# Spreading the third pair's decay factors between two products of the first y, from an eight-row operand on GpSimd's queue

## Chip, cores and metric

One NeuronCore of one Trainium2 chip runs the whole kernel. The metric is the device time in microseconds (us) of one execution. It was taken in three runs, and one further execution was recorded by the hardware profiler. Engine names are those of the profile: PE is TensorE (PEld its weight loads), DVE VectorE, ACT ScalarE, POOL GpSimd, SP SyncE, which here only issues DMAs.

## What is computed

A chunked state-space product (Mamba-2) is followed by a feed-forward block with a sigmoid-type gate. The reference, cut to what matters (4 batches b, 8 heads h, 768 steps, chunks of 32 in the reference, head size 32, state size 16; then 3072 tokens of width 256, hidden width 2048):

```python
log_a = np.log(np.clip(a, 1e-06, 1.0))
for c in range(nc):
    cum = np.cumsum(la, axis=-1)
    L = np.exp(cum[:, :, :, None] - cum[:, :, None, :]) * causal
    CB = np.einsum('bhin,bhjn->bhij', Cc, Bc)
    y_intra = np.einsum('bhij,bhjd->bhid', CB * L, xc)
    y_inter = np.einsum('bhin,bhnd->bhid', Cc, state) * decay_to_i
    y[:, :, sl] = y_intra + y_inter
    state = decay_full * state + sum_j(Bc x xc * decay_from_j)
x = y.transpose(0, 2, 1, 3).reshape(3072, 256)
h = x @ w_in                      # 256 x 2048
g = h * (1.0 / (1.0 + np.exp(-1.702 * h)))
out = g @ w_out                   # 2048 x 256
```

`x, a, B, C` are float32; `w_in` and `w_out` are float64 and come into the kernel as pairs of 32-bit words.

## The kernel before

The 3072 tokens are worked off in six groups of 512 (TG), each of four blocks of 128 steps (a batch has six such blocks, NC = 6; CG = 4). Two blocks make a pair, so that there are twelve pairs and a group has two (PG = 2). A block is cut into two chunks of 64. All engines follow one written order: the program is emitted in the order in which it shall run, and `in_order` at the end pins each engine's instructions to it. Nothing is rescheduled afterwards, so what is late on an engine holds up everything behind it.

**Decay factors.** For a pair, VectorE makes L, the running products of a within a chunk, with one scan along the free axis. The scan needs a, with a zero at each chunk's first step, copied to every partition ("spread"). Pairs 0 and 1 go another way: log a is summed up (`cum`), TensorE forms the differences and ScalarE takes the exp. Pairs 3 and later read a spread by DMA from `scratch` (`spread`). The third pair, number PG = 2, is spread by TensorE. `pick_a` (ScalarE, L375) copies a's rows twice, scaled by a column of zeros and ones, so that each quarter of the partitions holds two heads and zero elsewhere. `fan_all` (L421) then multiplies with ones, eight products into the four PSUM banks `ab2`, which `decay_fanned` scans (L464).

For the state's decay from the batch's start, `since`, the rows of a are needed once per state row. For batch 0's first four blocks they come from the exp of `cum`; for its last two, `fan_since` has TensorE repeat them by a matrix of zeros and ones, `whose` (L515), and repeat each chunk's first value too (L544), and `since_fanned` scans these from PSUM (L555, L557). For the later batches a DMA copies the rows to 16 partitions each (`spread_rows`), `clip_rows` clips them on VectorE and moves the first values with GpSimd, and `decay_rows` scans.

**Order of the start.** TensorE: products that keep it busy (L454), the masks (L562), the differences (L568), a few small products as padding (`pads(11)`, L446), transposes (L641), the scores of pairs 0 and 1 (L696) with the rows for `since` (L526) between them, the chunk sums (L727), a filler (L1178), then the first y: the chunk products of pair 0 (L850), a filler product of 192 columns into the area `idle` (L1178), the chunk products of pair 1 (L850) and those with the state (L836). ScalarE copies y to `yT` (L870).

**First hidden layer.** `hidden(0, f)` for f from 0 to 15 (L907) multiplies yT with block f of w_in: two products of 512 columns, each of which TensorE runs as two records with a weight load each; ScalarE applies Silu. After block f the entries of `in_hidden[0][f]` are emitted: the work of other engines for later. There the float64 words are turned into float32 weights piece by piece: `fields` (L192, L195) and `rounded` (L208) on VectorE, `clamp` on ScalarE (L203, L204), `join` on VectorE (L222, L228). `narrow(i)` does this for piece i. Piece 4 holds blocks 8 to 11, piece 5 blocks 12 to 15, later pieces w_out. After block 5 `store_a` clips a and stores it to `scratch`, after block 7 comes `pick_a(2)`, after block 9 `fan_all(2)`. In `narrow(4)` stands the clip of a's last two blocks (L360, L366, L367), in `narrow(6)` the scan `since_fanned`.

**Then** group 0 is multiplied with w_out (`project_all`, L1004), with the scores, chunk sums and y of pairs 2 and 3 between (L696, L727, L836, L850, at places 10 and 15). `turn` transposes B and C of pairs 2 and 3 by TensorE, and `since_start` (L681) multiplies C with `since` into CsT. From group 1 on both layers are done with fewer products by Strassen-Winograd's scheme (L962, L972, L1067, L1074; sums on VectorE at L930 and L1094, copies on ScalarE at L967, Silu at L939).

**PSUM.** `bank` takes one of four single banks in turn, used by h, o, tp, A and the rows; `area` is one tile of four banks, used in turn by ab0, cb0, `idle`, ab2, cb2 and so on.

**DMA queues.** SyncE issues nearly all DMAs in program order. Its semaphores are used in a ring of eight: an issue waits until the DMA eight issues earlier has landed. `rows_a` loads a's 32 rows (batch and head) four times, once for each quarter of the partitions (L279), behind the pieces of w_in.

**GpSimd** makes the constant masks at the start (`pick0`, `ident`, `below`, `same`, `pick`, `whose`), the masked C of pairs 0 and 1 (L664, `mask_first`), CsT of pairs 0 and 1 (L681), and small moves later. The second L664 waits for a memset on VectorE (L663) that stands behind the first `fields`.

Of the kernel before, what the change touches and what calls it, by code (L numbers as in the profile page):

```python
# [8 lines left out]
FP32 = mybir.dt.float32  # L9
# [3 lines left out]
ALU = mybir.AluOpType  # L13
# [3 lines left out]
P = 128  # L17
# [18 lines left out]
def kernel(  # L36
# [70 lines left out]
        "p (c s) -> p c s", c=NC)  # L107
    az0 = ffn.tile([P, TG // 2], FP32, tag="b", name="az0").rearrange("p (c s) -> p c s", c=2)
    cum = const.tile([P, 2, P], FP32, name="cum")
    w_in = const.tile([P, NF, NK, P], FP32, name="w_in")  # L110
# [164 lines left out]
    def rows_a(t, queues):  # L275

        e = t.shape[1] * P
        for r in range(R):
            queues[r % len(queues)].dma_start(  # L279
                out=t[32 * r:32 * r + 32].rearrange("p c s -> p (c s)"),  # L280
                in_=a.rearrange("b h s -> (b h) s")[:, :e])

# [72 lines left out]

    starts, fans, flat = {}, {}, {}

    def clip(t, name):
# [3 lines left out]
        if name:  # L362
            starts[name] = const.tile([P, t.shape[1], 2], FP32, name=f"starts{name}")
        first = t.rearrange(by_chunk, s=2)[:, :, :, 0]
        if name:
            nc.vector.tensor_copy(starts[name], first)  # L366
        nc.vector.memset(first, 0.0)  # L367

    def pick_a(p):

        b, c = divmod(2 * p, NC)
# [17 lines left out]
    for i, n, head in ((0, 1, PG), (1, 2, PG), (0, 0, 1)):  # L389
        t = whose[32 * i:32 * i + 32, n:n + 1]  # L390
        nc.gpsimd.affine_select(out=t, in_=t, pattern=[[-1, 1], [-head, NH], [0, N]],
                                compare_op=ALU.is_equal, fill=0.0, base=-max(n - 1, 0),
                                channel_multiplier=1)
# [98 lines left out]
    def clip_rows(b):  # L492
        t = raf[b]
        nc.vector.tensor_scalar(out=t, in0=t, scalar1=1e-6, scalar2=1.0,
                                op0=ALU.max, op1=ALU.min)
        first = ssd.tile([P, NC, P], FP32, tag="first", name=f"first{b}", bufs=1)
        nc.gpsimd.memset(first, 0.0)
        f, t0 = (v.rearrange(by_chunk, s=2)[:, :, :, 0] for v in (first, t))
        nc.gpsimd.tensor_copy(f, t0)
        nc.gpsimd.memset(t0, 0.0)  # L500
        firsts[b] = first

    def decay_rows(b):

        t, first = raf.pop(b), firsts.pop(b)
        since[b] = ssd.tile([P, NC, P], FP32, tag="since", name=f"since{b}")
        nc.vector.tensor_tensor_scan(
            out=since[b].rearrange("p c s -> p (c s)"), data0=t.rearrange("p c s -> p (c s)"),
            data1=first.rearrange("p c s -> p (c s)"),
            initial=0.0, op0=ALU.mult, op1=ALU.add)  # L510

    def fan_rows(t, c0, c1, o):

        o = o[:, :(c1 - c0) * P]
        nc.tensor.matmul(out=o, lhsT=whose[:32, 0].rearrange("p h n -> p (h n)"),  # L515
                         rhs=t[:32, c0:c1].rearrange("p c s -> p (c s)"), start=True,
                         stop=True, tile_position=(0, 0), skip_group_check=True)
        return o

    def since_first():  # L520

        since[0] = ssd.tile([P, NC, P], FP32, tag="since", name="since0")
        rows = [bank(f"rows{p}")[:, :2 * P] for p in range(PG)]
        for p in range(PG):
            at = slice(32 * p, 32 * p + 32)
            nc.tensor.matmul(out=rows[p],  # L526
                             lhsT=whose[at, 1 + p].rearrange("p h n -> p (h n)"),
                             rhs=cum[at].rearrange("p k s -> p (k s)"), start=True, stop=True,
                             tile_position=(32 * p, 0), skip_group_check=True)
        for p in range(PG):  # L530
            nc.scalar.activation(since[0][:, 2 * p:2 * p + 2].rearrange("p c s -> p (c s)"),
                                 rows[p], AF.Exp)

    def drops():
# [3 lines left out]
                1).to_broadcast([P, Q * D, 2 * CG - 1]))  # L538

    def fan_since():  # L540
        o = bank("rows4")
        t = fanned["rows"] = fan_rows(az, CG, NC, o)
        f = fanned["starts"] = o[:, 2 * P:2 * P + 2 * (NC - CG)]
        nc.tensor.matmul(out=f, lhsT=whose[:32, 0].rearrange("p h n -> p (h n)"),  # L544
                         rhs=starts[1][:32].rearrange("p c s -> p (c s)"), start=True, stop=True,
                         tile_position=(0, 0), skip_group_check=True)

    fanned = {}

    def since_fanned():  # L550

        t, f = fanned["rows"], fanned["starts"]
        first = ssd.tile([P, NC, P], FP32, tag="first", name="first0", bufs=1)[:, CG:]
        nc.gpsimd.memset(first, 0.0)
        nc.vector.tensor_copy(first.rearrange(by_chunk, s=2)[:, :, :, 0],  # L555
                              f.rearrange("p (c s) -> p c s", s=2))
        nc.vector.tensor_tensor_scan(  # L557
            out=since[0][:, CG:].rearrange("p c s -> p (c s)"), data0=t,
            data1=first.rearrange("p c s -> p (c s)"), initial=0.0, op0=ALU.mult, op1=ALU.add)

# [34 lines left out]
    def bank(name):  # L595
        return ps.tile([P, 4 * P], FP32, tag="ff", name=name)
# [205 lines left out]
    def finish(pairs, steps=range(2)):  # L802
# [98 lines left out]
    def hidden(g, f):  # L901
        j, i = divmod(f, 2)
        if i == 0:
            block(g, j)
        h = bank(f"h{g}_{f}")
        for k in range(NK):
            nc.tensor.matmul(out=h, lhsT=w_in[:, f, k], rhs=yT[g][:, k], start=(k == 0),  # L907
                             stop=(k == NK - 1), skip_group_check=True)

        nc.scalar.activation(gT[g, j][:, i], h, AF.Silu, scale=GELU_SCALE)  # L910
# [285 lines left out]
    fields(0)  # L1196
    mask_first(1)
    to = area("cb0")
    pads(11, to[:, 0])
    turn_back()  # L1200
# [11 lines left out]
    for i in range(2, 6):  # L1212
        fetch(i)
    rows_a(az, (nc.sync,))
    since_start(1, nc.gpsimd)
# [21 lines left out]
    def store_a():  # L1237
        clip(az[:BH, :CG], 0)
        for i, side in enumerate(SIDES):
            nc.sync.dma_start(out=scratch[:, i].rearrange("c r i -> r c i"), in_=az[:32, :, side])  # L1240
# [224 lines left out]
```

## Time and profile before

| what | value |
|---|---|
| median of 3 runs | 348.57 us (348.41 to 349.02) |
| profiled execution | 348.56 us |
| its span, first to last instruction | 346.5 us |
| PE busy | 341.6 us, 99% of the span |
| PEld, DVE busy | 269.1 us (78%), 255.5 us (74%) |
| ACT, POOL busy | 154.9 us (45%), 15.3 us (4%) |
| DMA | 25.92 MB, mean 75 GB/s |
| granted TensorE clock | 1.000 |

The time lies 2.06 us over the span, for what surrounds the first and the last instruction. The busy table of the page adds up instructions of an engine; an engine can be busy all the time and still not set the end, so the table is read beside the chain, which follows the work that ended last back to its start. The timeline lists instructions in order: start, duration, engine, line, operation, output and inputs, count, and in brackets the idle time of the engine before it with what ended that. Instructions of a kind that follow each other stand in one row, and a row's duration runs to the end of its last one. TensorE's instructions are pipelined, so that what counts there is the distance between starts.

### The profile page before, as it was taken

Reading aid. Unit: us, or ns where it says so; the run is one execution under the profiler, and the core shown is the slowest. Engines: PE = TensorE matmul, PEld = TensorE weight load, DVE = VectorE, ACT = ScalarE, POOL = GpSimd, SP = SyncE. Lnnn points to the kernel's source line nnn. Section 1 sums busy time; section 2 is a strip of 40 time slices with the busy share of each in tenths; the row PEclk is TensorE's granted clock in tenths of the full one; section 3 lists DMA queues with packets and bytes.
Section 4 is the critical chain, followed back from the end, with each engine's and each line's share of the span. In section 5 each row is a group of like instructions: output and inputs, shape, how many; then the busy total and the mean of one; then the engine's idle time right before and its main releaser. Section 6 shows DMA issues by size and latency. Waiting matters only on the chain.

```text
span 346.5 us, 8120 instructions
## 1 busy us (share of the span) xinstructions
PE 341.6 (99%) x3378; PEld 269.1 (78%) x3378; DVE 255.5 (74%) x484; ACT 154.9 (45%) x352; POOL 15.3 (4%) x42
## 2 busy tenths in 40 slices
PE   8999999999999999999999999999999999999996
PEld 6634444555788888888888888888888888899996
DVE  5889899998799998857996667788464654465463
ACT  4788771407354323754342554432554321554320
POOL 7300010300000100000000000000000000000000
PEclk9999999999999999999999999999999999999999
DMA  6599899645726100435703037400000400000402
GB/s 159 134 294 222 229 234 123 152 70 97 120 59 125 45 0 11 69 91 97 120 24 53 2 80 122 61 0 3 0 4 3 61 2 0 0 2 0 62 0 61
DMA packets 89981, 25.92 MB, mean 75 GB/s; under 512 B 73433, under 2 KB 87129, under 8 KB 89945
## 3 DMA queue, kind: packets, MB, share of 16 engines
q1 hardware_dynamic: 89112, 24.88, 36.0%
q8 instruction: 26, 0.43, 0.6%
q10 hardware_dynamic: 832, 0.52, 0.5%
q14 instruction: 11, 0.08, 0.1%
HBM read 22.15 MB, written 3.24 MB: 73 GB/s over the span
## 4 chain that ended last, share of the span: by engine, by line
PE 96%; DVE 2%; ACT 1%; issue 0%
PE acc L1067 28%; PE X L962 19%; PE Y L972 14%; PE h L907 9%; PE o L1004 8%; PE acc L1074 7%; PE cb L696 2%; PE y L850 2%; PE y L836 1%; PE A L727 1%; PE ab L568 1%; PE busy L454 1%; DVE L L707 1%; PE ab L562 0%; DVE p L222 0%; DVE steps L749 0%
## 5 line engine op out<-in xcount | busy, mean ns | idle before, releaser
L967 ACT ACTIVATE ac<-X 128x256 f32<-128x256 f32 x76 | 29.1, 383 | 81.5 <-PE X L962 80.8
L1067 PE MATMUL acc<-mg,mw 128*128 128x256 f32 x192 | 54.5, 379 | 0.0
L1094 DVE TENSOR_TENSOR gT<-Y,ac 128x512 f32<-128x512 f32 x38 | 26.2, 689 | 38.1 <-PE Y L972 32.5
L939 ACT ACTIVATE gT<-gT 128x512 f32<-128x512 f32 (+1 forms) x76 | 38.9, 519 | 29.5 <-DVE gT L1094 28.9
L962 PE MATMUL X<-my,mi 128*128 128x256 f32 x152 | 45.2, 380 | 0.0
L1067 PEld LDWEIGHTS acc<-mg,mw 128*128 128x128 f32 x192 | 36.5, 190 | 5.0
L1094 DVE TENSOR_TENSOR gT<-Y,b 128x256 f32<-128x256 f32 x38 | 15.8, 419 | 28.6 <-PE Y L972 28.6
L907 PE MATMUL h<-yT,w_in 128*128 128x512 f32 x80 | 35.6, 597 | 0.7 <-ACT yT L870 0.5
L1067 PE MATMUL acc<-gT,w_out 128*128 128x256 f32 x128 | 35.5, 379 | 0.0
L962 PEld LDWEIGHTS X<-my,mi 128*128 128x128 f32 x152 | 28.0, 190 | 4.1 <-ACT ac L967 0.4
L907 PEld LDWEIGHTS h<-yT,w_in 128*128 128x128 f32 x80 | 14.8, 189 | 19.1 <-issue 15.4
L1004 PE MATMUL o<-gT,w_out 128*128 128x512 f32 x64 | 28.3, 595 | 0.0
L930 DVE TENSOR_TENSOR mg<-gT 128x512 f32<-128x512 f32 x40 | 27.2, 681 | 0.0
L1067 PEld LDWEIGHTS acc<-gT,w_out 128*128 128x128 f32 x128 | 24.2, 190 | 3.4 <-ACT yT L885 0.2
L967 ACT ACTIVATE b<-X 128x256 f32<-128x256 f32 x38 | 14.6, 383 | 21.0 <-PE X L962 20.6
L962 PE MATMUL X<-yT,w_in 128*128 128x256 f32 x76 | 23.2, 389 | 0.0
L972 PE MATMUL Y<-yT,w_in 128*128 128x256 f32 x76 | 22.7, 381 | 0.0
L972 PE MATMUL Y<-my,mi 128*128 128x256 f32 x76 | 22.7, 380 | 0.0
L972 PE MATMUL Y<-yT,mi 128*128 128x256 f32 x76 | 22.5, 379 | 0.0
L962 PE MATMUL X<-my,w_in 128*128 128x256 f32 x76 | 22.4, 379 | 0.0
L1004 PEld LDWEIGHTS o<-gT,w_out 128*128 128x128 f32 x64 | 11.8, 190 | 13.6 <-issue 13.2
L411 DVE TENSOR_TENSOR_SCAN L<-a,idents 128x1024 f32<-128x1024 f32 x9 | 20.5, 2277 | 0.4 <-DMA a<-scratch 0.4
(159 smaller groups left out, 549.7 us busy)
## 6 DMA issues: line engine op xcount, KB each, us to landing
a<-scratch SPq DMA_DIRECT2D x18, 256.0 KB, 5.1
bits<-in_moe_w_out_dram SPq DMA_DIRECT2D x8, 512.0 KB, 7.2
x<-in_x_dram SPq DMA_DIRECT2D x24, 128.0 KB, 3.7
out_dram<-ob SPq DMA_DIRECT2D x40, 64.0 KB, 2.0
bits<-in_moe_w_in_dram SPq DMA_DIRECT2D x8, 256.0 KB, 4.6
bits<-in_moe_w_in_dram SPq DMA_DIRECT2D x4, 512.0 KB, 10.6
b<-in_B_dram SPq DMA_DIRECT2D x20, 64.0 KB, 3.3
af<-in_a_dram SPq DMA_DIRECT2D x3, 384.0 KB
```

The costliest lines, as they stand in the source:

```text
L411: nc.vector.tensor_tensor_scan(out=L, data0=ra[p].rearrange("p k e -> p (k e)"), data1=idents.rearrange("p h i -> p (h i)"), initial=0.0, ...
L696: nc.tensor.matmul(out=s["cb"][side, r, k].rearrange("p (q i) -> p q i", q=Q), lhsT=BT[rows, k, side], rhs=CT[rows, k, :, side], start=Tru ...
L907: nc.tensor.matmul(out=h, lhsT=w_in[:, f, k], rhs=yT[g][:, k], start=(k == 0), stop=(k == NK - 1), skip_group_check=True)
L930: nc.vector.tensor_tensor(out=t[:, 0:2], in0=B[:, :, 1], in1=B[:, 0], op=ALU.subtract)
L939: nc.scalar.activation(o, i, AF.Silu, scale=GELU_SCALE)
L962: nc.tensor.matmul(out=s["X"], lhsT=lhsT, rhs=rhs, start=i == "1", stop=i == "4", skip_group_check=True)
L967: nc.scalar.activation(copy, s["X"], AF.Copy)
L972: nc.tensor.matmul(out=o, lhsT=lhsT, rhs=rhs, start=s.pop("new", False), stop=i != "5", skip_group_check=True)
L1004: nc.tensor.matmul(out=o[c], lhsT=w_out[:, c, f], rhs=gT[g, f // 2][:, f % 2], start=(f == 0), stop=(f == NF - 1), skip_group_check=True)
L1067: nc.tensor.matmul(out=acc[g][0][i][:, cols], lhsT=w, rhs=h[:, cols], start=(j == 0 and k == 0 and (i, 0) in begins), stop=(j == NF // 2 - ...
L1074: nc.tensor.matmul(out=o[k] if type(o) is list else o[:, cols], lhsT=h[:, cols], rhs=w, start=(j == 0 and (i, k) in begins), stop=(j == NF ...
L1094: nc.vector.tensor_tensor(out=o, in0=v, in1=w, op=ALU.add)
```

## The change

The eight products that spread pair 2's factors move from behind hidden block 9 to the first y, in the place of the filler product `idle`. For this their operand must be there about 20 us earlier, and it is made in another way: `az1` is filled with ones, and one DMA on GpSimd's queue brings the eight rows of batch 0's last two blocks to every sixteenth partition. `clip(az1)` clips it on VectorE ahead of the first `fields`, and `pick_a` reads it with a column `pick1`, which VectorE sums from `ident` (L399's kind), in place of GpSimd's `pick`. `pick_a` is now emitted behind `mask_first(1)`.

What `fan_since` did with TensorE goes: `since` for batch 0's last two blocks now comes from `spread_rows(0)` (a DMA of 128 KB), `clip_rows(0)` after block 8 and `decay_rows(0)` in the place of `since_fanned`. The matrix `whose` loses a third, `pick` is gone, a is loaded once and not four times, `store_a` clips all 768 columns at once. Hidden blocks 10 to 12 are multiplied in two halves of 256 columns each. Two of the eleven padding products go.

```diff
 def narrow(i):
-        if i == 4:
-            clip(az[:, CG:], 1)
         if i == 6:
-            since_fanned()
+            decay_rows(0)
...
     def spread_rows(b):
-        raf[b] = raw.tile([P, NC, P], FP32, tag="af", name=f"af{b}", bufs=1)
+        c = CG if b == 0 else 0
+        raf[b] = raw.tile([P, NC, P], FP32, tag="af", name=f"af{b}", bufs=1)[:, c:]
         nc.sync.dma_start(out=raf[b].rearrange("p c s -> p (c s)"),
-                          in_=a[b].unsqueeze(1).to_broadcast([NH, N, S]))
+                          in_=a[b, :, c * P:].unsqueeze(1).to_broadcast([NH, N, S - c * P]))
...
     def pick_a(p):
-            nc.scalar.activation(X[:, :, q], az[:, c:c + 2], AF.Copy, scale=pick[:, b, q:q + 1])
+            nc.scalar.activation(X[:, :, q], az1, AF.Copy, scale=pick1[:, q:q + 1])
+    APART = P // NH
+    nc.gpsimd.memset(az1, 1.0)
+    nc.gpsimd.dma_start(
+        out=az1.rearrange("(h e) c s -> h e (c s)", e=APART)[:, 0], in_=a[0, :, TG:])
...
-    pick = picker("pick", NB, 1, NH)
-    whose = const.tile([32 * PG, 1 + PG, NH, N], FP32, name="whose")
+    whose = const.tile([32 * PG, PG, NH, N], FP32, name="whose")
...
+    pick1 = const.tile([P, Q], FP32, name="pick1")
+    nc.vector.tensor_reduce(
+        out=pick1, in_=ident.rearrange("p (r q e) -> p q r e", q=Q, e=APART)[:, :, :, 0],
+        op=ALU.add, axis=AX.X)
...
     def fan_all(p):
         for r in range(R):
             fan(p, r, ab[:, r])
-        fan_since()
...
                 if n:
-                    dense(3, area("idle")[:, 0])
+                    fan_all(PG)
                 intra(n, p)
...
     def hidden(g, f):
+        n = 2 if g == 0 and f in range(10, 13) else 1
         for k in range(NK):
-            nc.tensor.matmul(out=h, lhsT=w_in[:, f, k], rhs=yT[g][:, k], start=(k == 0),
-                             stop=(k == NK - 1), skip_group_check=True)
+            for c in range(n):
+                cols = slice(c * TG // n, (c + 1) * TG // n)
+                nc.tensor.matmul(out=h[:, cols], lhsT=w_in[:, f, k], rhs=yT[g][:, k, cols],
+                                 start=(k == 0 and c == 0), stop=(k == NK - 1),
+                                 skip_group_check=True)
...
     turn_first("B")
+    clip(az1)
...
     mask_first(1)
+    pick_a(PG)
     to = area("cb0")
-    pads(11, to[:, 0])
+    pads(9, to[:, 0])
...
-    rows_a(az, (nc.sync,))
+    nc.sync.dma_start(out=az[:BH].rearrange("p c s -> p (c s)"),
+                      in_=a.rearrange("b h s -> (b h) s"))
+    spread_rows(0)
...
     def store_a():
-        clip(az[:BH, :CG], 0)
+        clip(az[:BH])
...
-    at(in_hidden[0], 7, lambda: pick_a(PG))
-    at(in_hidden[0], 9, lambda: fan_all(PG))
+    at(in_hidden[0], 8, lambda: clip_rows(0))
```

On each engine this leaves the other instructions in their order. VectorE's row for `since` loses the copy L555 ahead of the scan, and the scan reads SBUF in the place of PSUM.

More of the change, by code (lines that the diff above doesn't have):

```diff
@@ L108 @@
     az0 = ffn.tile([P, TG // 2], FP32, tag="b", name="az0").rearrange("p (c s) -> p c s", c=2)
+    az1 = const.tile([P, NC - CG, P], FP32, name="az1")
     cum = const.tile([P, 2, P], FP32, name="cum")
@@ L354, with clip @@
         data1=cum.rearrange("p k s -> p (k s)"), initial=0.0, op0=ALU.mult, op1=ALU.add)
-    starts, fans, flat = {}, {}, {}
-    def clip(t, name):
+    fans, flat = {}, {}
+    def clip(t):
         nc.vector.tensor_scalar(out=t, in0=t, scalar1=1e-6, scalar2=1.0,
                                 op0=ALU.max, op1=ALU.min)
[L362 to L367, printed above, removed]
+        nc.vector.memset(t.rearrange(by_chunk, s=2)[:, :, :, 0], 0.0)
     def pick_a(p):
-        b, c = divmod(2 * p, NC)
+        assert divmod(2 * p, NC) == (0, CG)
         X = ffn.tile([P, 2, DM], FP32, tag="ob", name=f"X{p}")
@@ L385 @@
         fill=0.0, base=N - 1, channel_multiplier=-1)
-    pick = picker("pick", NB, 1, NH)
-    whose = const.tile([32 * PG, 1 + PG, NH, N], FP32, name="whose")
+    whose = const.tile([32 * PG, PG, NH, N], FP32, name="whose")
     nc.gpsimd.memset(whose, 1.0)
[L389 to L392, printed above, removed]
+    for n in range(PG):
+        t = whose[32 * n:32 * n + 32, n:n + 1]
+        nc.gpsimd.affine_select(out=t, in_=t, pattern=[[-1, 1], [-PG, NH], [0, N]],
+                                compare_op=ALU.is_equal, fill=0.0, base=-n,
                                 channel_multiplier=1)
@@ L495, in clip_rows @@
                                 op0=ALU.max, op1=ALU.min)
-        first = ssd.tile([P, NC, P], FP32, tag="first", name=f"first{b}", bufs=1)
+        first = ssd.tile([P, NC, P], FP32, tag="first", name=f"first{b}", bufs=1)[:, -t.shape[1]:]
         nc.gpsimd.memset(first, 0.0)
@@ L505, in decay_rows @@
         t, first = raf.pop(b), firsts.pop(b)
-        since[b] = ssd.tile([P, NC, P], FP32, tag="since", name=f"since{b}")
+        if b:
+            since[b] = ssd.tile([P, NC, P], FP32, tag="since", name=f"since{b}")
         nc.vector.tensor_tensor_scan(
-            out=since[b].rearrange("p c s -> p (c s)"), data0=t.rearrange("p c s -> p (c s)"),
+            out=since[b][:, -t.shape[1]:].rearrange("p c s -> p (c s)"), data0=t.rearrange("p c s -> p (c s)"),
             data1=first.rearrange("p c s -> p (c s)"),
             initial=0.0, op0=ALU.mult, op1=ALU.add)
[L512 to L518, printed above, removed]
     def since_first():
@@ L538, in drops @@
                 1).to_broadcast([P, Q * D, 2 * CG - 1]))
[L540 to L559, printed above, removed]
     def mask(t, new):
```

11 lines of the change are left out of this document (3 added, 8 removed).

## The prediction

> **What bounds the kernel now.** First the page's chain that ended last, to see which engine carries the end; then the timeline, at the place the spread leaves and at the place it goes to; then the other engines' rows, to see who would be late next. In the two first lines (engine lines of the page's busy table and of its chain) the reader is to see that TensorE is busy for 99% of the span and carries 96% of the chain.
>
> ```profile
> PE 341.6 (99%) x3378; PEld 269.1 (78%) x3378; DVE 255.5 (74%) x484; ACT 154.9 (45%) x352; POOL 15.3 (4%) x42
> ...
> PE 96%; DVE 2%; ACT 1%; issue 0%
> ```
>
> The chain in order of time says where the other 4% lie: VectorE and ScalarE carry it from 12.08 to 21.74 us, and after 21.74 it is TensorE alone.
>
> ```profile
> 12.08 2.03 DVE L L707 x2
> 14.35 1.23 DVE steps L749
> 17.70 0.69 DVE idents L342
> ...
> 20.99 0.70 DVE w_in L228
> 21.74 14.00 PE h L907 x32
> 37.10 10.50 PE h L907 x24
> ```
>
> So work taken from TensorE counts after 21.74 and is free before it. The spread stands in the part that counts (TensorE's timeline), between the tenth and the eleventh hidden block:
>
> ```profile
> 34.72 1.02 PE L907 MATMUL h<-yT,w_in 128*128 128x512 f32 x2
> 35.67 0.69 PE L421 MATMUL ab<-X,ones 32*64 32x256 f32 x16
> 36.28 0.69 PE L515 MATMUL rows<-az,whose 32*128 32x256 f32 x2
> 36.82 0.28 PE L544 MATMUL rows<-starts,whose 32*128 32x4 f32 x2
> 37.03 1.55 PE L907 MATMUL h<-yT,w_in 128*128 128x512 f32 x3
> ```
>
> The place it goes to lies in the part that is free:
>
> ```profile
> 14.77 0.59 PE L1178 MATMUL idle<-ones 128*128 128x192 f32 x2
> 15.29 1.10 PE L850 MATMUL y<-L,x 64*32 64x64 f32 x64
> ```
>
> **Removed from TensorE's path.** The last h record before the spread starts at 35.15, the first after it at 37.03: 1.88 us, where two h records in a row start 0.43 apart (weight loads at 22.70, 23.13, 23.56). That is 1.45 us. The record at 37.03 is followed 0.53 later instead of 0.43, as after every change of tile shape: 0.10 more. Sum 1.55 us: 0.61 the spread (35.67 to 36.28), 0.75 the rows and starts products, the rest the two changes of shape.
>
> **Added at the first y.** The idle product took 14.77 to 15.29, 0.52 us; the spread took 0.61 where it stood. Both change the shape away from 64x32 and back, so +0.1 us. It is hidden by a wait that is there: h for block 2 needs w_in from VectorE, and TensorE's weight load of 21.73 came after 0.99 us idle, where 0.24 is usual and about 0.33 us of matmul time was lost. TensorE at 14.77 also waits for the same thing as before (the score banks, read by the weighing, ended 14.43). The two pads taken out (11 to 9, 0.07 us) stand before a product that waits for ScalarE (9.40): nothing. If the cover were gone, the spread would cost its 0.1.
>
> **Three hidden blocks in two halves (10 to 12).** Twelve records of 512 columns become 24 of 256. The row for 256 columns is L1067: four records in 0.86 us, 0.215 each, twice that is 0.43, and its weight loads take 190 ns, which fits under 215. Cost 0.03 us at most; the upper end, loads not hidden, is excluded by that row.
>
> **ScalarE's two copies with scale (L375, 0.91 us)** move from 33.59 to behind the exps that end at 10.17. There the next instruction started at 11.34 after 1.17 us idle (waiting for TensorE's rows L526). 0.91 fits with 0.26 to spare: nothing.
>
> **VectorE early.** Added: one reduction (0.13, like L399) and the clip of the eight-row operand (0.28 and 0.06, the same rows at 32.88 and 33.44). The reduction falls into 1.25 us idle before 6.78. The clip falls into the 0.61 us that VectorE waited at 9.32 for weights, so 0.27 is left. But GpSimd's masking L664 runs from 7.91 to 8.95, and the profile shows the two engines in each other's way: L195 took 1.31 us beside GpSimd's fill, where its median is 0.69, and that fill took 1.14 where the others took 0.74.
>
> ```profile
> 45.91 1.14 POOL L497 MEMSET first<- 128x768 f32 x1 [32.41 <-DVE since L557]
> ...
> 46.28 1.31 DVE L195 TENSOR_SCALAR m<-bits 128x1024 uint32<-128x1024 uint32 x1
> ```
>
> A clip that waits until 8.95 ends at 9.29, just in time; one slowed by as much as that row (twice) is 0.3 late. Bounds 0 and 0.3; I take 0.1. Behind the clip stand fields (L192), the memset at 10.03, for which GpSimd's second masking waits, for that the second score product (11.28, no slack), for that the weighing at 12.08. All of this is on the path, so lateness costs one for one.
>
> **GpSimd and its queue.** Gone: the picker of eight columns (4.58 to 6.04, 1.46 us) and a third of a fill (0.14). Added ahead of `same`: a fill like `same`'s (0.31) and one DMA issue c. No row shows a DMA issue on GpSimd. Nearest rows: 0.47 us for one on SyncE's queue, 2.07 for GpSimd's longest instruction (L499); I take 1.0, between them. `same` then ends at 4.63 + 0.31 + 1.0 = 5.9, its two reductions before 6.3, and the transposes start at 6.78 as before. Free up to c = 1.5, and to 1.8 with VectorE's 0.27. GpSimd's first masking (7.91) has 1.46 + 0.14 - 0.31 = 1.3 us in hand, and TensorE takes it 1.0 later.
> The transfer is issued at about 3.55 and must land by 8.98. DMAs in the profile take from 1.6 (least median of the DMA issues) to 5.1 us (first x half, behind the weights). With c: 6.1 to 9.7 for c = 1.0, and 10.7 for both upper ends. I take 3 to 4: no wait; upper end 1.75 us late.
>
> **SyncE's queue.** Four issues of 96 KB (20.69 to 24.41) become one of 96 and one of 128 KB: two issues and 160 KB less, everything behind is earlier. The first landed 9.8 us after issue, so by 31.5; the clip of the new rows comes at 34.8 on VectorE. The next rows transfer (46.92) must now wait for the scan that reads the old rows, which ended at 45.78: no wait. GpSimd's two small instructions after that clip have nothing behind them before 45.9.
>
> **VectorE in the hidden blocks.** Gone: 0.61 (32.88 to 33.49) and the copy L555, some 0.1. Added: clip 0.28, and 0.14 for 768 columns in place of 512. The 0.38 wait at 36.75 for ScalarE goes, as ScalarE is 0.9 freer. VectorE is about 0.6 us earlier, and stays so, as its rows have no gap to 66.
>
> **Who is late next.** TensorE comes 1.55 earlier, VectorE 0.6. The tightest product after that is the third pair's gain (L727, 66.71), whose second bank VectorE frees with CsT:
>
> ```profile
> 65.42 0.43 DVE L681 TENSOR_TENSOR CsT<-tp,since 128x256 f32<-128x256 f32 x1
> ...
> 66.71 0.79 PE L727 MATMUL A<-x,Be 64*32 64x64 f32 x56
> ```
>
> CsT ends at 65.85 - 0.6 = 65.25, TensorE wants 66.72 - 1.55 = 65.17: 0.1 to 0.15 us of wait. Weights are looser: w_in for block 12 (VectorE 38.17) against 40.56, w_out for block 12 (69.3) against 70.97.
>
> **Sum.** -1.55 + 0.03 + 0.13 + 0.1 = -1.3 us. The profiled execution took 348.56 (span 346.5 and 2.06 around it), the median is 348.57: forecast **347.3 us**. 0.2%, 0.70 us, is about what a measurement of this kernel tells from no change.
>
> **Rivals.**
> 1. *VectorE becomes the bound* at 66. If it is not earlier at all (a GpSimd copy in its way, a clip that costs more), CsT still ends at 65.85 and TensorE loses 0.7 of the 1.55: 347.9. For: VectorE is 9.65 of 10 us busy from 60 to 70. Against: its removed rows are larger than the added. 0.13.
> 2. *The operand comes late by GpSimd's queue: slower.* Place: VectorE's clip before fields at 9.32. It decides from 1.3 us of lateness, a landing after 10.3. Both upper ends give 348.56 - 1.3 + 1.75 = 349.0; with c also stretched by VectorE as L195 was (1.9 times 2.07 is 3.9), landing is at 12.6, 3.6 late: 350.8. VectorE works at 3.13, 4.00 and 4.77 beside that issue; against: these three last 0.3 to 0.7 us each. 0.12, time about 350.
> The Trainium skill (SBUF — State Buffer, section "SBUF: two separate sides") speaks for this rival: descriptors of a DMA issued from GpSimd are written by GpSimd's own cores, which are locked out while VectorE runs an operation that takes both ports, so such a DMA waits. Its example goes from about 0.62 to 3.1 us; the same 2.5 us added here, an estimate from that page, would land it at the edge. The pair L195 and L497 agrees that the two block each other; no run here shows it for a DMA yet.
> 3. *It doesn't do what it says:* the gap at 35.67 was needed anyway, because ScalarE or a weight wait fills it. Then 348.5. Against: h block 10 waits for nothing in the built program, and block 11's ScalarE wait has 1.6 in hand. 0.07.
>
> Forecast (346.9 to 347.7): 0.68. Faster by over 0.2% (below 347.87): it and half of rival 1, 0.74. Within: the other half, rival 3 and the near end of rival 2, 0.14. Slower: 0.12. Range: 346.9 (no wait, no clip cost, 0.1 below) to 348.6 (rivals 1 and 3, rival 2 up to its turning point).
>
> **What would show it.** h records 0.43 or 0.215 apart through 34 to 37, and a L727 about 1.4 us earlier; w_in at 21.74 unmoved; the clip of az1 over before 9.32; ScalarE's two copies between 10.2 and 11.3. Wrong if fields start later than 9.6, if w_in for block 2 moves past 22, or if a weight load of h, o or A shows a VectorE wait over 0.3 between 35 and 85.

## The result and the profile after

The changed kernel takes 346.68 us (median of 6, 346.43 to 347.67) beside 348.48 us for the kernel before (6, 348.24 to 349.02): a ratio of 0.9951, 95% interval 0.9937 to 0.9964. The forecast was 347.3 with a range from 346.9; the time is 0.2 us below it. The direction was right; the gain, 1.8 us, is larger than the 1.3 forecast. 0.09 of the 0.2 is the yardstick: the forecast started from 348.57 for the kernel before, which takes 348.48 here.

The profiled execution of the changed kernel is the slowest of the six (347.67 us, span 345.9). Its busy table and its chain:

```profile
PE 339.2 (98%) x3380; PEld 270.2 (78%) x3380; DVE 256.1 (74%) x484; ACT 155.1 (45%) x352; POOL 16.7 (5%) x40
...
PE 92%; DMA 3%; SPq 2%; DVE 1%; issue 0%; ACT 0%; POOL 0%; DVEq 0%
```

TensorE still carries the end, but a transfer has entered the chain. VectorE's and TensorE's timelines show where:

```profile
27.28 0.69 DVE L193 TENSOR_SCALAR p<-bits 128x1024 uint32<-128x1024 uint32 x1 [1.10 <-DMA bits<-in_moe_w_in_dram]
```
```profile
25.50 3.17 PE L878 MATMUL h<-yT,w_in 128*128 128x512 f32 x7
29.52 1.96 PE L878 MATMUL h<-yT,w_in 128*128 128x512 f32 x4 [0.85 <-DVE w_in L229]
```

In this one execution a piece of w_in landed late, VectorE stood 1.10 us and TensorE lost 1.02. The other five lie 0.8 to 1.2 us lower. So the change is read from a later profile of the same kernel without that wait (e8_again2 below: 346.75 us, span 345.0). There the hidden blocks stand behind each other without a break, where the spread and the rows products had stood from 35.67 to 37.03:

```profile
32.96 5.76 PE L878 MATMUL h<-yT,w_in 128*128 128x512 f32 x20
```

Comparing the start of one and the same TensorE record in the traces of before and of e8_again2 gives the account of the gain. Positive is later:

| record | before | after | later by |
|---|---|---|---|
| first product with the state in the first y (L836, now L804) | 16.32 | 16.71 | +0.39 |
| h, first record on w_in's block 2 | 21.74 | 21.80 | +0.06 |
| h, the record behind it | 22.27 | 22.23 | -0.04 |
| transpose behind the hidden blocks (L611, now L579) | 47.43 | 45.86 | -1.57 |
| X at 117 (L962, now L934) | 117.56 | 115.88 | -1.68 |
| X at 204 | 203.94 | 202.21 | -1.73 |
| end of the execution | 348.56 | 346.75 | -1.81 |

So 0.10 us goes at 21.8: before, the record behind the wait for w_in came 0.53 after the first, and now it comes 0.43 after it. 1.53 go between 22.3 and 47. 0.11 goes at 117, where a weight load had waited 0.43 for ScalarE's ac and now waits 0.31. The rest is 0.05, at the end of the small products ahead of 204, and 0.08 behind TensorE's last record. In the trace of e14_again3 (below, 347.08 us) the middle stretch is the same, 22.53 to 46.16, again 1.53 shorter; its start is 0.26 later than before, so these two executions differ mainly there.

### The profile page after: what moved, and what is told of

Same layout as the page of the kernel before. It is cut to its first block, busy times and chain, and to the rows that moved or that the text cites. A ratio compares the mean times of both kernels' runs of the same rounds, so it can differ in the third digit from the quotient of the medians.

```text
span 345.9 us, 8116 instructions
## 1 busy us (share of the span) xinstructions
PE 339.2 (98%) x3380; PEld 270.2 (78%) x3380; DVE 256.1 (74%) x484; ACT 155.1 (45%) x352; POOL 16.7 (5%) x40
## 4 chain that ended last, share of the span: by engine, by line
PE 92%; DMA 3%; SPq 2%; DVE 1%; issue 0%; ACT 0%; POOL 0%; DVEq 0%
PE acc L1039 28%; PE X L934 19%; PE Y L944 14%; PE o L976 8%; PE acc L1046 7%; PE h L878 7%; DMA bits<-in_moe_w_in_dram 3%; PE y L818 2%; PE cb L664 2%; SPq L181 1%; PE y L804 1%; PE A L695 1%; PE ab L536 1%; DMA az<-in_a_dram 1%; POOL CsT L649 0%
## 5 line engine op out<-in xcount | busy, mean ns | idle before, releaser
L934 PE MATMUL X<-my,mi 128*128 128x256 f32 x152 | 45.2, 380 | 0.0
L878 PE MATMUL h<-yT,w_in 128*128 128x512 f32 (+1 forms) x92 | 35.5, 541 | 1.4 <-DVE w_in L229 0.9
L878 PEld LDWEIGHTS h<-yT,w_in 128*128 128x128 f32 x92 | 17.2, 190 | 18.2 <-issue 12.8
L934 PEld LDWEIGHTS X<-my,mi 128*128 128x128 f32 x152 | 28.0, 190 | 4.0 <-ACT ac L939 0.3
L934 PE MATMUL X<-yT,w_in 128*128 128x256 f32 x76 | 23.2, 389 | 0.0
L934 PE MATMUL X<-my,w_in 128*128 128x256 f32 x76 | 22.5, 380 | 0.0
```

Of the source, the lines that this page charges most:

```text
L878: nc.tensor.matmul(out=h[:, cols], lhsT=w_in[:, f, k], rhs=yT[g][:, k, cols], start=(k == 0 and c == 0), stop=(k == NK - 1), skip_group_ch ...
L934: nc.tensor.matmul(out=s["X"], lhsT=lhsT, rhs=rhs, start=i == "1", stop=i == "4", skip_group_check=True)
```

## The experiments

All stand beside the kernel before on the same chip: 348.72 us (28 executions) for the first four, 348.62 (26) for e5 to e8, 348.63 (23) for e9 to e12, 348.75 (23) for the last two.

**The changed kernel again** (e1_again, e8_again2, e14_again3; no edit).

> The changed kernel once more, as the yardstick of this call. Theory A (the gain is TensorE's own time taken off its path between hidden blocks 9 and 10, 1.55 us, and some 0.2 us by which the start ended earlier): 1.7 to 1.9 us under the kernel before, ratio 0.995, and in the trace the h records of blocks 9 and 10 are 0.43 us apart. Theory B (the gain beyond the 1.3 us forecast is chance of the runs): 1.2 to 1.5 us. The 1.0 us that TensorE lost at 28 us in the profiled execution, while VectorE waited for the fifth piece of w_in, should be absent if it is chance, and there again if the new transfers make that piece late.

> The changed kernel unchanged, to stand beside the three others on the same chip and to have a third profile of it: 0.995 of the kernel before; TensorE's tenth to thirteenth hidden block without a gap; and, if the stalls of 1.02 us at 28 (on VectorE's w_in, which waits for a transfer) and 0.9 at 21 were of single executions, neither of them, a span of 344.9.

> The changed kernel unchanged, beside fewer_pads on the same chip: median 346.7 to 347.1, some executions 0.6 to 1 us above the lowest; the profile either without a gap at 21 us or with one of 0.3 to 1 us at the 961st instruction.

Measured: 347.06, 346.76 and 347.03 us; ratios 0.9966 (0.9945 to 0.9987), 0.9940 (0.9919 to 0.9961), 0.9945 (0.9916 to 0.9974). The gain holds, but single executions reach 349 and one 351.27. The profile of the last shows a wait of TensorE with no releaser (0.95 us up to 21.93, taken up again below), then three waits between 83.3 and 85.9 us, 0.93 us put down to VectorE and 0.56 and 0.33 to transfers of x, and behind these half the granted clock from 86.4 to 89.8.

**The spread put back behind block 9** (e3_spread_back).

```
-                    fan_all(PG)
+                    dense(3, area("idle")[:, 0])
...
+    at(in_hidden[0], 9, lambda: fan_all(PG))
```

> The spread goes back behind hidden block 9 and the filler product back into the first y; all else as changed (operand early, since by DMA, halves). Theory A: 0.61 us of products and 0.2 us for two changes of shape come back onto TensorE's path, 0.7 to 0.8 us slower than the changed kernel, so 1.0 to 1.1 us under the kernel before. Rival (the spread costs as much at the first y as it did at its old place, and the gain is that of the rows and starts products alone): equal to the changed kernel within 0.2 us.

Measured: 347.75 us, 0.69 above e1_again. Its timeline has the spread back in the row of h:

```profile
33.23 2.31 PE L878 MATMUL h<-yT,w_in 128*128 128x512 f32 x5
35.47 0.69 PE L418 MATMUL ab<-X,ones 32*64 32x256 f32 x16
36.08 2.64 PE L878 MATMUL h<-yT,w_in 128*128 128x256 f32 x11
```

From 35.47 to 36.08 are 0.61 us; against e8_again2 block 10 stands 0.71 further behind block 9 there and the next record another 0.10. That is the forecast's 0.61 and its two changes of tile shape.

**Two products of the removed rows put back behind block 9** (e10_rows_again).

```
+    def rows_again():
+        o = bank("rows4")
+        heads = whose[:32, 0].rearrange("p h n -> p (h n)")
+        for to, rhs in ((o[:, :2 * P], az1[:32].rearrange("p c s -> p (c s)")),
+                        (o[:, 2 * P:2 * P + 4], az1[:32, 0, :4])):
+            nc.tensor.matmul(out=to, lhsT=heads, rhs=rhs, start=True, stop=True, ...)
+    at(in_hidden[0], 9, rows_again)
```

> The changed kernel with two products put back behind hidden block 9, of the shapes of the rows and starts products that the change took out (32 rows by 128, 256 columns and 4 columns); nothing reads them, and the spread stays at the first y. The forecast's term: 0.75 us of products and 0.2 for two changes of tile shape, so TensorE is 0.9 to 0.95 us later from block 10 on in the trace: a time of about +0.9 us on the changed kernel, ratio 0.997. Rival: part of that is taken up later by a wait (VectorE's third pair at 66): less than 0.5 us at 70 us. The stream of instructions moves by eight places; if a stall of TensorE without a releaser comes or goes, it is read off by itself.

Measured: 348.08 us, ratio 0.9984 (0.9970 to 0.9997). The products stand where they stood and nothing takes them up later:

```profile
33.26 3.17 PE L878 MATMUL h<-yT,w_in 128*128 128x512 f32 x7
36.36 0.81 PE L1227 MATMUL rows<-az,whose 32*128 32x256 f32 x4
37.10 1.56 PE L878 MATMUL h<-yT,w_in 128*128 128x256 f32 x6
```

Against e8_again2 block 10 stands 0.84 further behind block 9 here and the next record another 0.10: 0.94, where 0.9 to 0.95 was expected. The 0.2 for the changes of shape is in both experiments, so the parts add up to 0.61 + 0.74 + 0.2 = 1.55. The profiled execution lost 0.7 more at 12 us on a transfer of x, which is not the edit's.

**No halves** (e2_no_halves and, for a second profile, e12_no_halves2).

```
-        n = 2 if g == 0 and f in range(10, 13) else 1
+        n = 1
```

> Hidden blocks 10 to 12 in one product of 512 columns each, as before the change. Theory A: the halves cost 0.03 us at most, so this is within 0.15 us of the changed kernel. Rival: the halves give something (a weight or a bank comes in time because of them, or the place of later instructions in TensorE's stream matters); then this is 0.3 us or more slower.

> no_halves once more for a second profile: its profiled execution was the fastest of twelve (347.94), the others lie 1 us higher. Theory P: besides the stall at 149 (present again, 1.0 to 1.3 us) a second one without a releaser near 18 to 22 us, or VectorE's wait for a piece of w_in at 27 us. Rival: the stall at 149 is absent, so it was of that execution alone.

Measured: 348.94 us, ratio 1.0002 (0.9980 to 1.0023); the second, a single execution, 348.3. The whole gain is gone, though up to 147 us both traces are as early as the changed kernel's. The loss that the traces show stands in the first dense burst of small products after that, in both profiles at one place. It is 1.1 to 1.25 of the 1.9 us between the medians of e2 and e1_again; both profiled executions were faster than e2's median, and what the slower ones lost besides isn't shown. First e2, then e12, then the changed kernel (e8_again2):

```profile
149.67 0.77 PE L818 MATMUL y<-L,x 64*32 64x64 f32 x54 [1.09 <-issue]
```
```profile
147.78 0.99 PE L818 MATMUL y<-L,x 64*32 64x64 f32 x74
150.01 0.78 PE L818 MATMUL y<-L,x 64*32 64x64 f32 x54 [1.25 <-issue]
```
```profile
147.72 1.52 PE L818 MATMUL y<-L,x 64*32 64x64 f32 x128
```

The break is behind the same record in both, the 3521st of TensorE counted from the start, with products, weight loads and the semaphore and drain instructions that the trace has (54 in all). The page's queue 8 points to what TensorE waits for:

```profile
q8 instruction: 26, 0.43, 0.5%
```

26 transfers of 16 KB of instructions each. One of them starts at 147.30 in e2 and takes 1.01 us, TensorE breaks off at 148.57 and goes on at 149.67. In e12 it is 147.78, 0.93 and 150.01. In the changed kernel the transfer comes at 144.40, ahead of the burst (146.94). Without the halves 24 fewer instructions stand ahead of this place (20 fewer than in the kernel before), so a block of 256 instructions lies almost whole in the burst and is used up before the next has come: in e12 130 products and as many weight loads start between 147.00 and 148.55 us, where 2.2 us go by from the transfer's start until TensorE goes on. e12 also has a break of 0.32 us without a releaser at 21.12, behind the 961st record.

**The count put back by other means.** Two edits to tell the place in the stream from the halves. The first gives the 24 instructions back ahead of the first mask (e5_count_back), the second halves other blocks (e9_halves_13).

```
-        for i in range(n):
+        for i in range(n + 6):
+            w = 2 if i < 2 else 1
...
-        n = 2 if g == 0 and f in range(10, 13) else 1
+        n = 1
```
```
-        n = 2 if g == 0 and f in range(10, 13) else 1
+        n = 2 if g == 0 and f in range(13, 16) else 1
```

> As no_halves (hidden blocks 10 to 12 in one product each), but with six more small products ahead of the first mask: the four idle products of 192 columns (768 columns) become ten of 64 and 128 (768 columns), so that TensorE's later instructions stand at the same count from the start as in the changed kernel. Theory P (no_halves lost its time to the place in TensorE's instruction stream: its transfer of 16 KB of instructions came at 147.30 instead of 145.25 us and TensorE stood 1.09 us with nothing to wait for at 148.6, while the halves as such cost and give nothing): the transfer is back at 145.3 and the stall at 149 is gone, the trace is within 0.2 us of the changed kernel's from block 13 on, and the time is that of the changed kernel, ratio about 0.995. Rival Q (the halves themselves are what counts, by the weights' or the banks' timing): the stall at 149 stays, or the loss of some 1.3 us is elsewhere, ratio about 1.000.

> The changed kernel with the halves at hidden blocks 13 to 15 instead of 10 to 12: the same number of TensorE's instructions, the same products, only three blocks later. Theory P (the place in the instruction stream): from block 16 on the stream stands as in the changed kernel, so its transfers of 16 KB come where they come there (145 us), no stall at 149, time that of the changed kernel, ratio 0.994 to 0.995. Rival Q (halving blocks 10 to 12 as such is worth something, as no_halves lost 1.9 us): as no_halves, ratio about 1.000.

Measured: e9 347.03 us, ratio 0.9951 (0.9932 to 0.9969), its transfer at 144.47 and the burst unbroken. So it is not which blocks are halved. e5 took 352.19 us, ratio 1.0094 (1.0065 to 1.0124). Its expected time failed, and for the same reason: the break at 149 is gone (the transfer at 149.49 lies ahead of the burst, which starts at 152.04 here), though no block is halved: it is the count. But the early part of the stream is now shifted too, and a block ends inside the first y:

```profile
17.59 1.03 PE L805 MATMUL y<-CsT,S 32*64 32x64 f32 x52
21.67 0.39 PE L805 MATMUL y<-CsT,S 32*64 32x64 f32 x4 [3.05 <-issue]
22.00 3.57 PE L879 MATMUL h<-yT,w_in 128*128 128x512 f32 x4
```

The break follows the 961st record, and 3521 less 961 is ten times 256. The transfer it waits for comes at 19.18, among w_in's pieces (the 16 DMA engines full from 18 to 25 us). Behind the break the granted clock is 0.5 from 21.8 to 25.2, and four h records take twice their time: 1.6 us more. The masks behind the ten idle products also start 1.6 us later than behind the four, and 1.2 of that is left at 14 us.

**One more use of that count** (e13_fewer_pads). The changed kernel reaches the 961st record at 20.4 to 21.4 us, and in e1_again, e12_no_halves2 and e7_two_issues (below) it breaks off there for 0.95, 0.32 and 0.59.

```
-    pads(9, to[:, 0])
+    pads(1, to[:, 0])
...
-        n = 2 if g == 0 and f in range(10, 13) else 1
+        n = 2 if g == 0 and f in range(9, 16) else 1
```

> The changed kernel with one pad instead of nine ahead of the third stage's first product (16 records less, 32 of TensorE's instructions with their weight loads, at 9 us where TensorE waits for ScalarE), and seven hidden blocks in halves instead of three (9 to 15 instead of 10 to 12: 32 instructions more), so that from block 16 on every instruction has its old count. Theory: TensorE's instructions come in blocks of 256, and one block ends with the 961st weight load or product of the trace, which the changed kernel reaches at 20.4 to 21.4 us, 2 to 2.5 us after its next block was fetched in an undisturbed execution and before it is there in others (gaps of 0.95 and 0.6 us without a releaser in two of its profiles or near copies). With 32 instructions less that place lies some 7 us later, so no such gap can come at 21 us: no run above 347.5 but by other causes (w_in's transfer at 27 us, a clock drop), the lowest as the changed kernel's (346.5), median 346.6 to 346.8, ratio 0.994 to 0.995, and the fetch beside 18 us is at the same time while the boundary is at 27 to 28 us. Rival: the gaps at 21 us have another cause (w_in, ScalarE): gaps and the scatter stay as they are; or the missing pads cost clock or start time: 0.3 us or more slower at 12 us.

Measured: 347.06 us, ratio 0.9948 (0.9918 to 0.9978), 346.78 to 350.16. The profile has no such gap, but the median missed the 346.6 to 346.8 expected: it is that of e14_again3 (347.03), and three of twelve lie above 347.5 all the same. So the scatter of single executions is not of this place alone. Late pieces of w_in, late instructions and clock drops were each seen once or twice; how often each comes stays open.

**The operand later** (e6_late_operand): the forecast's second rival made true. The DMA issue goes behind the masks of whose.

```
     nc.gpsimd.memset(az1, 1.0)
-    nc.gpsimd.dma_start(out=az1..., in_=a[0, :, TG:])
...
+    nc.gpsimd.dma_start(out=az1..., in_=a[0, :, TG:])
```

> The changed kernel with GpSimd's DMA issue for the eight rows moved from ahead of the fills of same to behind the masks of whose (from 3.88 to about 6.4 us). Nothing is left out. Theory T (the start up to 21.5 us is a chain through VectorE, so what comes late by the operand comes late at the end): issue to landing was 3.1 us, so it lands at 9.5 to 10.2 instead of 7, VectorE's clip starts 1.0 to 1.7 later than 8.46, w_in for block 2 and everything behind it is 0.9 to 1.6 later: ratio about 0.999. If VectorE's transposes beside the issue block its descriptors as the forecast's second rival has it: landing at 11 to 12, 2.5 to 3.5 late, ratio 1.002 to 1.005. Theory U (the wait for w_in at 21 us has slack, as the transfers of w_in set it): within 0.3 us of the changed kernel, 0.995.

Measured: 349.58 us, ratio 1.0023 (1.0002 to 1.0044), 2.8 above e8_again2. VectorE's clip waits for the transfer, 2.55 us later than in e8_again2 (8.48), and the windows (length, then busy time of PE, PEld, DVE, ACT and POOL, then the granted clock, the DMA share and GB/s) show the price of the wait on TensorE:

```profile
11.03 0.29 DVE L354 TENSOR_SCALAR az<-az 128x256 f32<-128x256 f32 x1 [2.66 <-DMA az<-in_a_dram]
```
```profile
11.00:12.00 1.00, 0.00 (x0) 0.00 (x0) 0.90 (x4) 0.51 (x2) 0.00 (x0) 1.00 0.16 23
12.00:13.00 1.00, 0.00 (x0) 0.00 (x0) 1.00 (x5) 0.97 (x4) 0.70 (x1) 0.52 0.00 0
13.00:14.00 1.00, 0.60 (x24) 0.60 (x32) 0.89 (x1) 0.95 (x1) 1.00 (x2) 0.50 0.00 0
...
18.00:19.00 1.00, 1.00 (x64) 0.81 (x55) 0.96 (x4) 0.84 (x3) 0.00 (x0) 0.57 0.80 191
```

TensorE's second score product is 2.15 later than in e8_again2, and in the 6.8 us at half clock this grows to 3.9 at the spread (18.72 for 14.82). e8_again2 then has a break of 0.25 us that this trace has not (see the next section), and from the first hidden block to the third pair the difference is 3.45: 3.3 at the end.

**Two issues on GpSimd's queue** (e7_two_issues).

```
-    nc.gpsimd.dma_start(out=az1..., in_=a[0, :, TG:])
+    for c in range(2):
+        nc.gpsimd.dma_start(out=az1...[:, 0, c], in_=a[0, :, TG + c * P:TG + (c + 1) * P])
```

> The changed kernel with the operand's DMA on GpSimd's queue made as two of half the columns: two issues. Doubles the price of the issue and nothing else. Forecast's term (an issue is free up to 1.5 us in all): with 0.74 each, GpSimd's same ends at 7.1 instead of 6.36, VectorE's part at 7.2, the transposes start 0.6 to 0.75 later than 6.68, and the weighing and w_in for block 2 with them: +0.4 to +0.7 us, ratio about 0.997. Rival: the chain from the transposes has slack, or the second issue is cheap (0.1 to 0.2): ratio 0.995 and the transposes move by less than 0.2.

Measured: 347.12 us, ratio 0.9950 (0.9927 to 0.9973), 0.36 above e8_again2. The second issue costs 0.51 and not 0.74 (two take 1.28, one 0.77), the transposes start at 7.02 instead of 6.69, and the first y is 0.2 later. The profile's loss of 0.8 at 22 us is a break at the 961st record, not the issue.

**The operand on ScalarE's queue** (e4_act_queue): no issue on GpSimd, one on ScalarE behind C's four.

```
+    nc.gpsimd.memset(az1, 1.0)
...
+    nc.scalar.dma_start(out=az1..., in_=a[0, :, TG:])
...
-    nc.gpsimd.dma_start(out=az1..., in_=a[0, :, TG:])
```

> The eight-row operand comes on ScalarE's queue behind C's rows, its fill of ones first on GpSimd; all else as changed. Theory A: GpSimd's issue (0.74 us in the profile) is hidden, so no difference within 0.15 us. Rival (the issue on GpSimd delays same, its reductions, and with them the transposes and fields): this is 0.2 us or more faster, with the transposes at the same time or earlier and fields before 9.1. It may also be slower where ScalarE's queue delays C's rows or the exps.

Measured: 349.18 us, 347.28 to 352.25, ratio 1.0020 (0.9991 to 1.0049). The issue itself is dearer there, and ScalarE's copy of cum stands behind it:

```profile
4.46 1.15 ACTq L292 DMA_DIRECT2D az<-in_a_dram  x1
5.73 0.42 ACT L348 ACTIVATE cum<-az 128x256 f32<-128x256 f32 x1 [2.06 <-DMA zC<-in_C_dram]
```

VectorE's scan of cum starts at 6.18 instead of 5.03, TensorE waits 1.1 for it, and the h records at 22 us are 0.8 later than in the changed kernel's first profile. Another 0.6 goes at 30 on a wait for w_in. Three of the twelve executions had a mean granted clock of 0.985 to 0.995, so the median says more than the queue alone.

**The kernel before with a transfer on GpSimd's queue** (e11_before_queue). The time around the span is 2.02 us in the kernel before and 1.73 to 1.74 in the changed one, and 2.02 in e4_act_queue.

```
+    nc.gpsimd.dma_start(out=spare, in_=a[0, :, :P])
     load(PG, "bc")
```

> The kernel before with one thing added: a transfer of eight rows of 128 on GpSimd's queue at about 22 us, where GpSimd has nothing to do; nothing reads it. Theory R (what lies around the span was 2.03 us in the kernel before, 1.74 in five kernels with one transfer on GpSimd's queue and 2.00 in act_queue, which has none: the queue itself makes the difference): around the span 1.74, span as before (346.5), time 348.3, ratio 0.999. Rival: it is something else of the change (the SyncE queue, the fills): around the span 2.03.

Measured: 348.89 us, ratio 1.0007 (0.9991 to 1.0023), around the span 2.02. The theory falls: a transfer on that queue is not what does it, and what does stays open. It hardly matters for the account: from TensorE's last record to the end of the execution it is 4.84 us in the profile of before and 4.75 in that of e8_again2.

## What the forecast had right, and which step failed

- *Removed from TensorE's path, -1.55.* Right: 1.53 between 22.3 and 47 us, with the halves' cost in it. The pieces were measured apart: the spread 0.61 with 0.1 at each change of shape (e3), the rows and starts 0.74 with 0.2 (forecast 0.75 and 0.2; e10).
- *Added at the first y, +0.1, hidden.* The price was right: the spread takes 0.62 us there (14.82 to 15.44) for the idle product's 0.52, and e10_rows_again needs 1.41 from the spread to the products with the state where e3_spread_back, with the idle product, needs 1.32. In e8_again2 a break comes on top:

```profile
14.82 0.69 PE L418 MATMUL ab<-X,ones 32*64 32x256 f32 x16
15.44 0.24 PE L818 MATMUL y<-L,x 64*32 64x64 f32 x1
15.93 0.84 PE L818 MATMUL y<-L,x 64*32 64x64 f32 x63 [0.25 <-issue]
```

 One product, then 0.25 us in which TensorE waits for nothing shown. It is the break of the experiments above once more: it stands behind the 705th record, 256 ahead of the 961st, and TensorE goes on 1.35 us after a 16 KB transfer (13.63 to 14.58) is over. The profiles of after (0.30), e7 (0.31) and e4 (0.08) have it behind the same record. Before, the products at this count start 0.23 apart too, so the one in e8_again2 (0.47) makes up 0.24 of the 0.39 by which the products with the state come later.

 The cover was larger than the forecast's 0.33, as the late record behind the wait (0.53 for 0.43) belongs to it. The weights' wait is still in the weight load's row, first before, then e8_again2, but holds up no product any more, since the record ahead holds TensorE until 21.80:

```profile
21.73 0.30 PEld L907 LDWEIGHTS h<-yT,w_in 128*128 128x128 f32 x2 [0.99 <-DVE w_in L228]
```
```profile
21.69 0.30 PEld L878 LDWEIGHTS h<-yT,w_in 128*128 128x128 f32 x2 [0.56 <-DVE w_in L229]
```

- *Halves, +0.03.* The cost is right (24 records in 5.18 us for 5.15). What the forecast did not see is that the 24 instructions matter: without them a break of 1.1 to 1.25 us comes at 149 (e2, e12), and no gain is left. The forecast gives no reason for the halves, so as far as it goes the missing break is luck.
- *ScalarE's copies, nothing.* Right: 10.04 to 10.97, the next instruction at 11.35.
- *VectorE's early clip, +0.1.* It took 0.58 instead of 0.28 beside GpSimd's masking, near the "twice" of the upper bound. But fields started at 9.27 (9.32 before) and the weights of block 2 were ready at 21.64 (21.68 before): the room held, and the 0.1 was not there.
- *GpSimd's issue, 1.0.* 0.77 and 0.30 of idle time ahead of it: 1.07. Landing 3.1 and 3.6 us after issue in two profiles (after, e8_again2): within 3 to 4. The transposes started at 6.69 (6.78 before). That an issue is free up to 1.5 us held for one; two, 1.58 with the idle time, delay the transposes by 0.33 (e7).
- *SyncE's queue.* Wrong in part, without an effect on TensorE that these traces show. The one issue of 96 KB took 3.13 us in e8_again2 and 3.56 in after, nearly as long as the old four (3.72), and the next left at 23.04 and 24.06. In e8_again2 the first piece of w_out leaves earlier (23.88 for 24.51) and a later one is later (46.49 for 45.64), so not everything behind is earlier.
- *VectorE 0.6 earlier, so a wait of 0.13 at the third pair.* **This is the step that failed.** VectorE is 1.0 earlier. The removed 0.61 was right; the copy L555 was 0.19 and not 0.1, the new clip and the longer one cost 0.33 and not 0.42, and the wait for ScalarE gave 0.46 and not 0.38. CsT therefore ends before TensorE comes (VectorE, then TensorE, in e8_again2):

```profile
64.42 0.42 DVE L649 TENSOR_TENSOR CsT<-tp,since 128x256 f32<-128x256 f32 x1
```
```profile
65.14 0.79 PE L695 MATMUL A<-x,Be 64*32 64x64 f32 x56
```

 CsT ends at 64.84, 0.30 ahead: no wait where the forecast has 0.13.
- *Sum.* -1.3 forecast, -1.81 measured from the profile of before to that of e8_again2. The difference of 0.5 is 0.13 (that wait), 0.14 (the start: 0.04 earlier instead of the clip's 0.10 later), 0.11 at 117, 0.05 ahead of 204 and 0.08 behind TensorE. The last three are the other fault: the sum ends at the third pair, and everything behind it was put at nothing without a reason, so that the lower edge, 346.9, lies 0.1 below the sum without that wait and without the clip's cost, and no lower. A range that knows only new waits lacks the old ones that end, as the one at 117 does in part. What the 0.05 and the 0.08 are was not tried.
- *Rivals.* The first (VectorE the bound at 66) is refuted by the lines above. The second did not come true, but e6 shows its price: 2.55 us of lateness of the clip cost 2.8 us of time (3.3 in the profiled execution), over the forecast's one for one, with 6.8 us at half clock in it. The Trainium skill (SBUF — State Buffer, section "SBUF: two separate sides") had VectorE's two-port operations lock out a GpSimd-issued DMA, with 2.5 us added by its example. Landing took 3.1 us, 3.6 and 4.9 from issue in after, e8_again2 and e6_late_operand, the last with transposes of VectorE beside it. This one is 1.3 to 1.8 more than the others, and whether by that rule or by the other transfers these runs can't tell. The third rival is refuted by e3 and e10.

## What to carry to other kernels

Time taken from the engine that sets the end comes through at full size, if each piece is read as a distance between neighbours' starts and the place it goes to has a wait behind it. Then follow the other engines to where they meet it again, in both directions: a range that holds only new waits forgets the old ones that end. And where TensorE runs hundreds of tiny products, count its instructions: adding or removing a few dozen far ahead can open or close a break (here of up to 3 us), which shows in the timeline as "issue" at a fixed count.

## What was unexpected of the hardware

- *TensorE's instructions arrive in blocks, and late.* Breaks without a releaser stood behind the 705th (0.08, 0.25, 0.30 and 0.31 us), the 961st (0.32, 0.59, 0.95 and 3.05) and the 3521st record (1.09 and 1.25), 256 and 2560 apart, and each ended 1.3 to 1.6 us after a transfer of 16 KB on queue 8 was over. The Trainium skill (Runtime: NRT & Kernel Launch, section "Instruction fetch mechanics") gives blocks of 16 KiB or 256 instructions, which agrees (256 is one of them and 2560 ten), and calls the cost of crossing a block's end mostly hidden, which these breaks do not bear out for dense bursts of small products or full DMA engines.
- *A break can halve the clock.* In e6's break (10.71 to 13.40) TensorE's granted clock fell to 0.5 at 12.04, 1.33 us after its last product, and stayed there until 18.86; with e5's (18.62 to 21.67) it was 0.5 from 21.80 to 25.21. Breaks of 1.25 us and less, alone, left it at 1.00; the three of e1_again close together (0.93, 0.56 and 0.33) were followed by 0.5 from 86.4 to 89.8. The stretches at half rate lasted 6.8, 3.4 and 3.4 us. The Trainium skill (TensorE: Matmul & The Clock Gate, section "What's actually happening") puts the return to half rate at an idle window of about 3.4 us that runs freely; the half rate in e6, 1.33 us into the break, is sooner than that figure.
- *The same issue differs by queue*: 0.77 us on GpSimd's, 1.15 on ScalarE's, in the same early microseconds.
